# Staging the loads, splitting the denominator off and halving the first chunks in a fused attention and MLP kernel

## The chip, the cores and the metric

The kernel runs on one core of a Trainium2 chip. A core has five engines that run side by side and meet only at semaphores: PE (matrix multiply, TensorE), DVE (VectorE), ACT (ScalarE), POOL (GpSimd) and SP, which here only issues transfers. Each engine takes its instructions in the order of its own queue. Transfers between device memory and the on-chip memory are issued by SP, ACT or POOL and run on 16 DMA engines that all three share. The metric is the device time of one execution in microseconds; lower is better.

## The reference

Inputs are q, k and v of shape (4 batches, 4 heads, 1088 positions, 32), two small sketch matrices S1 and S2 (8 x 32), and the MLP weights w_in (128 x 2048) and w_out (2048 x 128). All are float32.

```python
def phi(x):                       # 8 x 8 products of two sketches: 64 features
    a = einsum('rd,bhsd->bhsr', S1, x)
    b = einsum('rd,bhsd->bhsr', S2, x)
    return einsum('bhsi,bhsj->bhsij', a, b).reshape(*x.shape[:-1], 64)
q_p, k_p = phi(q), phi(k)
kv = einsum('bhsf,bhsd->bhfd', k_p, v)
z = sum(k_p, axis=2)
num = einsum('bhsf,bhfd->bhsd', q_p, kv)
den = einsum('bhsf,bhf->bhs', q_p, z) + 1e-6
x = (num / den) as 4352 tokens x 128 (heads side by side)
out = square(relu(x @ w_in)) @ w_out
```

Nothing of a batch's queries can be finished before all of its keys are summed, since `kv` and `z` run over all 1088 positions. The MLP then works token by token.

## The kernel before, in words

**The order.** A string, `ORDER`, lists some 500 operations by hand. A loop at the end calls them one by one, and each call pins its instructions, so every engine executes its own share of the list in the list's order. An item such as `R.0.3@A` is an operation, its indices and the engine (A for ACT, V for DVE, G for POOL). DMA loads at the top of the kernel are not pinned: the framework places them in their queue, and gives every DMA one of eight lanes (semaphores), so that a later DMA of a lane waits for the earlier one to land.

**Keys of batch b.** `kT` (L212, L218) transposes the loaded k on DVE. `ka` (L233) multiplies it by the sketches on PE, in two groups, 0 and 1, of 4 and 4.5 column blocks. `kc` (L251) copies the result from PSUM on ACT. `kp` (L262) forms the 64 products on DVE. `kv` (L280) sums products times v on PE, and in the same accumulation sums a 32 x 32 product of the two sketches (L290), from which the denominator weights come. `kt` (L302, L309) copies both sums out, `kr` (L315) transposes the first, and in the same operation a matmul with S2 (L324) turns the second into denominator weights. `kx` (L334) and `wc` (L338) put them into `KV` and `Wq`.

**Queries of batch b.** `qT` (L352, L358) transposes q on DVE. `qa` (L380) multiplies by `Wq`, which holds S1, the denominator weights and S2 side by side, in two halves. `qc` (L392) copies to SBUF. `dt`, `dr`, `da` (L400, L407, L412, L419) compute the denominator, its reciprocal and the divided sketch. `qf` (L432) forms the 64 products, `qp` (L445) transposes them. `nd` (L469) multiplies by `KV` on PE, `xe` (L484) casts the result to bfloat16.

**MLP.** Eight chunks of 512 tokens, two for each batch, and a ninth of 256 for the positions that are left over. For each chunk there are eight steps u: `M` (L492) multiplies by two blocks of w_in, `R` (L506 on ACT, L508 on DVE) takes the ReLU from PSUM, `S` (L515 on ACT, L517 on DVE) squares it, `O` (L527) multiplies by w_out and accumulates. `E` (L539) copies the sum out of PSUM and SP stores it (L545; the last chunk L555, in eight small DMAs on SP and ACT).

**Loads.** SP issues k and q of all four batches one after the other (L142, L143), with S1 ahead of them (L116). POOL issues v of batch 0 in four heads and two remainders (L131, L136), then w_in and w_out (L146, L148, converted to bfloat16 on the way), then v of the other batches.

Of the kernel before, what the change touches and what calls it, by code (L numbers as in the profile page):

```python
# [30 lines left out]

ORDER = """
kT.0 ka.0.0 kc.0.0@A ka.0.1 kc.0.1@A kp.0.0 kp.0.1 kv.0.0 kv.0.1 qT.0 kt.0@A kr.0 kx.0@A kT.1
wc.0 qa.0.0 qc.0.0@A qa.0.1 qT.1 qc.0.1@A ka.1.0 ka.1.1 kc.1.0@A dt.0.0@V dr.0.0 da.0.0@V
dt.0.1@V qf.0.0 dr.0.1 da.0.1@V kc.1.1@A qf.0.1 qp.0.0 qp.0.1 nd.0.0 kp.1.0 kv.1.0 xe.0.0@A
M.0.0 R.0.0@A M.0.1 kp.1.1 qT.2 kv.1.1 kt.1@A R.0.1@V S.0.0@V M.0.2 R.0.2@A kr.1 wc.1 S.0.1@V
kT.2 M.0.3 nd.1.0 xe.1.0@V kx.1@A R.0.3@A S.0.3@V S.0.2@A M.0.4 R.0.4@A M.0.5 qa.1.0 qa.1.1
qc.1.0@V R.0.5@A dt.1.0@V qc.1.1@A S.0.4@V dr.1.0 dt.1.1@V da.1.0@V dr.1.1 ka.2.0 ka.2.1 M.0.6
qf.1.0 S.0.5@A R.0.6@A M.0.7 R.0.7@A O.0.0 kc.2.1@A S.0.6@V O.0.1 O.0.2 da.1.1@G M.1.0 M.1.1
O.0.3 O.0.4 R.1.0@A M.1.2 qp.1.0 qf.1.1 qp.1.1 R.1.1@A S.0.7@V O.0.5 R.1.2@A S.1.0@V O.0.6  # L40
kc.2.0@A kp.2.0 M.1.3 M.1.4 R.1.3@A R.1.4@A kp.2.1 nd.2.0 S.1.1@V O.0.7 E.0@A M.1.5 R.1.5@A
S.1.2@V M.1.6 S.1.4@V O.1.0 kv.2.0 kv.2.1 xe.2.0@A R.1.6@A S.1.6@V O.1.1 M.2.0 kt.2@A R.2.0@A
S.2.0@A kr.2 O.1.2 S.1.3@V M.1.7 R.1.7@A wc.2 M.2.1 R.2.1@A kx.2@V qa.2.0 qa.2.1 qc.2.1@A kT.3
ka.3.0 S.1.5@A O.1.3 M.2.2 qc.2.0@V dt.2.0@V dr.2.0 da.2.0@V kc.3.0@A R.2.2@A dt.2.1@G M.2.3
R.2.3@A O.1.4 O.1.5 O.1.6 S.1.7@V O.1.7 qf.2.0 E.1@A S.2.1@V M.2.4 R.2.4@A M.2.5 R.2.5@A S.2.5@A
O.2.0 nd.3.0 dr.2.1 da.2.1@V ka.3.1 M.2.6 R.2.6@A M.2.7 R.2.7@A qf.2.1 kc.3.1@A qp.2.0 S.2.2@V
O.2.1 S.2.3@V O.2.2 O.2.3 xe.3.0@V S.2.4@V M.3.0 R.3.0@A M.3.1 kp.3.0 S.2.6@V O.2.4 O.2.5 O.2.6
S.2.7@V R.3.1@A M.3.2 O.2.7 M.3.3 qp.2.1 S.3.1@A kp.3.1 S.3.0@V E.2@A nd.4.0 R.3.3@A R.3.2@A
xe.4.0@V S.3.3@A kv.3.0 kv.3.1 M.3.4 S.3.2@V M.3.5 O.3.0 O.3.1 kt.3@A kr.3 qT.3 R.3.4@A kx.3@V
wc.3 M.4.0 R.4.0@V S.3.4@V R.3.5@A S.3.5@V M.4.1 R.4.1@A S.4.1@A qa.4.0 qc.4.0@A qa.3.0 qa.3.1  # L50
M.3.6 qc.3.0@V O.3.2 dt.3.0@V dr.3.0 R.3.6@A M.3.7 R.3.7@A O.3.3 O.3.4 S.4.0@V qc.3.1@A M.4.2
S.3.6@V da.3.0@G R.4.2@A M.4.3 R.4.3@A S.3.7@V O.3.5 dt.3.1@V dr.3.1 qf.3.0 qp.3.0 O.3.6 S.4.2@V
S.4.3@V O.3.7 E.3@A da.3.1@G qf.3.1 qp.3.1 M.4.4 dt.4.0@G nd.5.0 R.4.4@A M.4.5 M.4.6 xe.5.0@A
R.4.5@A R.4.6@A O.4.0 O.4.1 M.4.7 R.4.7@A S.4.4@V O.4.2 O.4.3 M.5.0 R.5.0@A M.5.1 R.5.1@V nd.6.0
M.5.2 xe.6.0@V S.4.5@A R.5.2@A S.4.6@V M.5.3 R.5.3@A S.5.0@V O.4.4 O.4.5 S.4.7@V dr.4.0 da.4.0@G
S.5.3@V M.5.4 R.5.4@A O.4.6 M.5.5 S.5.1@V R.5.5@A O.4.7 E.4@V M.5.6 S.5.5@V R.5.6@A S.5.2@V
qf.4.0 nd.7.0 xe.7.0@A M.5.7 R.5.7@A M.6.0 R.6.0@A O.5.0 O.5.1 S.5.4@V M.6.1 R.6.1@A O.5.2 M.6.2
R.6.2@A S.5.6@V O.5.3 O.5.4 M.6.3 S.5.7@V R.6.3@A qp.4.0 M.6.4 S.6.1@A O.5.5 R.6.4@V O.5.6 M.6.5
S.6.0@V O.5.7 M.7.0 R.6.5@A nd.8.0 E.5@V R.7.0@A M.6.6 M.7.1 S.6.2@V O.6.0 S.6.4@A S.6.3@V O.6.1
R.6.6@A S.6.6@A O.6.2 R.7.1@V M.7.2 R.7.2@A S.6.5@V M.6.7 xe.8.0@A O.6.3 O.6.4 O.6.5 S.7.1@V  # L60
M.7.3 R.7.3@A R.6.7@V S.6.7@V O.6.6 M.7.4 S.7.0@V S.7.2@V O.6.7 E.6@V R.7.4@A M.7.5 nd.8.1
R.7.5@A S.7.3@V M.7.6 S.7.5@V xe.8.1@A M.7.7 R.7.7@V O.7.0 O.7.1 O.7.2 R.7.6@A S.7.4@A M.8.0
M.8.1 S.7.7@V R.8.1@V R.8.0@A S.7.6@A O.7.3 O.7.4 M.8.2 M.8.3 S.8.1@V R.8.3@A S.8.0@A O.7.5
O.7.6 R.8.2@V S.8.2@V M.8.4 R.8.4@A M.8.5 R.8.5@V S.8.5@V O.7.7 E.7@A M.8.6 R.8.6@V M.8.7
S.8.3@A O.8.0 O.8.1 O.8.2 O.8.3 S.8.4@V O.8.4 R.8.7@A S.8.7@A S.8.6@V O.8.5 O.8.6 O.8.7 E.8@A
# [4 lines left out]
def kernel(  # L70
# [11 lines left out]
    nc = tc.nc  # L82
# [7 lines left out]
    W = 3 * r  # L90
# [10 lines left out]
    qab_pool = pool("qab", 3)  # L101
# [3 lines left out]
    r_pool = pool("r", 6)  # L105
    g_pool = pool("g", 6)
# [9 lines left out]
    nc.sync.dma_start(out=S12[:r, 0, :], in_=S1)  # L116
# [11 lines left out]
    def load_v(b):  # L128
        for h in range(H):
            vr = v[b, h].rearrange("(t j) d -> t j d", j=NJ)[:, : 4 * NLO, :]  # L130
            nc.gpsimd.dma_start(  # L131
                out=vraw[b][:, h, :NLO, :],
                in_=vr.rearrange("t (i l) d -> i t (l d)", i=4),
            )
        for j2 in range(2):
            nc.gpsimd.dma_start(  # L136
                out=vraw[b][32 * j2 : 32 * (j2 + 1), :, NLO, :],
                in_=v[b].rearrange("h (t j) d -> j t h d", j=NJ)[32 + j2],
            )

    for b in range(B):
        nc.sync.dma_start(out=kin_t[b], in_=k[b].rearrange("h (t j) d -> (h t) j d", j=NJ))  # L142
        nc.sync.dma_start(out=qin_t[b], in_=q[b].rearrange("h (t j) d -> (h t) j d", j=NJ))  # L143
    load_v(0)
    w_in_sb = consts.tile([128, C_TILES, 128], BF16)
    nc.gpsimd.dma_start(out=w_in_sb, in_=moe_w_in.rearrange("d (ct c) -> d ct c", c=128))  # L146
    w_out_sb = consts.tile([128, C_TILES, 128], BF16)
    nc.gpsimd.dma_start(out=w_out_sb, in_=moe_w_out.rearrange("(ct c) d -> c ct d", c=128))  # L148
    for b in range(1, B):
        load_v(b)  # L150


    mask = consts.tile([128, H], F32)
# [9 lines left out]
    dts = [consts.tile([128, 16, r + 1], F32, name=f"dt{i}") for i in range(3)]  # L163
# [5 lines left out]
    for i in (1, 3):  # L169
        pin(nc.vector.memset(kabs[i][64:, :, 4 * H :], 0.0))  # L170
        pin(nc.vector.memset(kps[i][64:, 4 * H :], 0.0))
    for b in range(B):
        pin(nc.vector.memset(vraw[b][64:, :, NLO, :], 0.0))
    KV = consts.tile([128, B, 2, 128], F32)
    qT_rem = consts.tile([128, B, 64], F32)
    pin(
# [5 lines left out]
    nc.tensor.transpose(  # L182
        T_ps[:, : 2 * r], S12.rearrange("r h d -> r (h d)"), ident[: 2 * r, : 2 * r]
# [10 lines left out]
    Wq = consts.tile([128, B, H, W], F32)  # L194
# [7 lines left out]
    T = {}  # L202

# [65 lines left out]

    def kv(b, gi, eng):  # L270
        if gi == 0:
            T["acc", b] = ps_m.tile([128, 512], F32, tag="m", name="acc_ps")
        acc = T["acc", b]
        t, s = T["kp", b, gi], T["kab", b, gi]
        P = 128
        for m in range(4 + gi):
            first, last = gi == 0 and m == 0, gi == 1 and m == 4
            for h in range(H):
# [3 lines left out]
                        vraw[b][:P, h, 4 * gi + m, :],  # L282
                        t[:P, m * H + h].rearrange("p i j -> p (i j)"),
                        start=first,
                        stop=last and h > 0,
                    )
                )
            a, b2 = (s[:P, x, m * H : m * H + H].rearrange("p h i -> p (h i)") for x in range(2))
            pin(
                nc.tensor.matmul(  # L290
                    acc[:32, 64:96],
                    b2,
                    a,
                    start=False,
                    stop=last,
                )
            )

    def kt(b, eng):
# [9 lines left out]
        pin(COPY[eng](Gs[:32, b], T["acc", b][:32, 64:96]))  # L309

    def kr(b, eng):
        T["kr", b] = t = ps_m.tile([128, 512], F32, tag="m", name="kr_ps")
        for f in range(2):
# [21 lines left out]

    def wc(b, eng):
        pin(
            nc.vector.tensor_tensor(  # L338
                out=Wq[:, b, :, r : 2 * r],
                in0=T["acc", b][:, 96:128].rearrange("p (h x) -> p h x", h=H),  # L340
                in1=mask[:, :, None].to_broadcast([128, H, r]),
                op=ALU.mult,
            )
        )
# [20 lines left out]
    def groups(b):  # L365
        return 4 if b < 4 else 2

    def qa(b, i, eng):
        T["qq", b, i] = t = ps_m.tile([128, 512], F32, tag="m", name="qab_ps")
        for m in range(groups(b)):  # L370
            for c in range(2):
# [4 lines left out]
                else:  # L376
# [4 lines left out]
                        t[64 * c : 64 * c + 64, m * H * W : (m + 1) * H * W],  # L381
# [6 lines left out]

    def qc(b, i, eng):
        n = groups(b) * H  # L390
# [206 lines left out]
```

## Time and profile before

| | us |
|---|---|
| three timed runs | 128.24, 129.75, 130.01 |
| their median | 129.75 |
| the profiled execution | 128.9 |
| its span on the core | 127.1 |
| DVE busy | 101.9 (80% of the span) |
| PE busy | 100.2 (79%) |
| ACT busy | 87.1 (69%) |
| POOL busy | 22.6 (18%) |

The span is the time from the first to the last instruction of the core. Busy time of PE is modelled, since its matmuls overlap in a pipeline; a busy PE need not be a PE at full speed. The chain that ended last is found by going back from the last instruction, at each step to whatever released it. By line it is 14% `M` (L492), 13% `O` (L527), 10% the loads of v and 9% squaring on DVE (L517). A row of the page gives the granted clock of PE over the span in 40 slices; it is at 9 tenths or more except in four slices between about 25 and 38 us, where it reads 6, 5, 5 and 7.

### The profile page before, as it was taken

What the parts mean: (1) busy time and instruction counts of PE and PEld (TensorE: products, weight loads), DVE (VectorE), ACT (ScalarE), POOL (GpSimd) and SP (SyncE); (2) the same over time, 40 slices, a digit from 0 to 9 for tenths busy, and PEclk for the clock granted to TensorE, in tenths of its full rate; (3) what the DMA queues carried; (4) which work ended last, traced back from release to release, by engine and by line L of the source; (5) the groups of instructions that cost most, each with busy time, mean ns of one, the idle gap of its engine ahead of it and who ended that gap; (6) DMA issues with size and microseconds to landing.
All of it is one profiled execution on the core that took longest, in us unless ns stands there. A gap on an engine that the chain in (4) does not pass through costs nothing.

```text
span 127.1 us, 4039 instructions
## 1 busy us (share of the span) xinstructions
PE 100.2 (79%) x1729; PEld 72.7 (57%) x1729; DVE 101.9 (80%) x187; ACT 87.1 (69%) x130; POOL 22.6 (18%) x38
## 2 busy tenths in 40 slices
PE   0062187307999998999998999999899999799920
PEld 0061086303576874878766687767376767669810
DVE  6359304999569999999999998999999799879800
ACT  4220003400449998989999997999799999599910
POOL 6934252049700120001000000240010000000000
PEclk9999999965579999999999999999999999999997
DMA  2999999965610000210030020002002003020121
GB/s 71 330 273 263 294 282 295 221 113 136 138 41 5 0 5 0 66 25 5 0 83 5 21 67 0 5 17 65 5 0 62 26 9 81 1 65 23 33 66 27
DMA packets 7953, 10.24 MB, mean 81 GB/s; under 512 B 4864, under 2 KB 5248, under 8 KB 7936
## 3 DMA queue, kind: packets, MB, share of 16 engines
q1 hardware_dynamic: 2896, 6.62, 18.0%
q0 software_dynamic: 4768, 3.30, 13.9%
q8 instruction: 13, 0.21, 0.8%
q10 hardware_dynamic: 272, 0.07, 0.2%
q14 instruction: 4, 0.03, 0.1%
HBM read 8.79 MB, written 2.23 MB: 87 GB/s over the span
## 4 chain that ended last, share of the span: by engine, by line
PE 39%; DVE 30%; DMA 10%; issue 8%; ACT 6%; POOL 2%; POOLq 0%; ACTq 0%; DVEq 0%
PE h_ps L492 14%; PE o_ps L527 13%; DMA v_in<-in_v_dram 10%; DVE g_sb L517 9%; PE acc_ps L280 5%; DVE qf L432 5%; PE nd_ps L469 4%; ACT r_sb L506 4%; DVE qp L445 4%; DVE kp L262 2%; DVE kT L212 2%; POOL v_in L131 2%; PE kr_ps L315 1%; DVE rec L412 1%; DVE den L407 1%
## 5 line engine op out<-in xcount | busy, mean ns | idle before, releaser
L506 ACT ACTIVATE r_sb<-h_ps 128x1024 bf16<-128x1024 f32 (+1 forms) x61 | 58.4, 1005 | 6.0 <-PE h_ps L492 4.7
L492 PE MATMUL h_ps<-xT,w_in_sb 128*128 128x512 bf16 (+1 forms) x144 | 38.8, 375 | 0.8 <-ACT r_sb L506 0.7
L527 PEld LDWEIGHTS <-g_sb 128*128 128x128 bf16 x544 | 33.1, 98 | 8.1 <-DVE g_sb L517 0.9
L527 PE MATMUL o_ps<-w_out_sb,g_sb 128*128 128x128 bf16 x544 | 36.6, 219 | 0.4 <-DVE g_sb L517 0.4
L517 DVE TENSOR_TENSOR g_sb<-r_sb 128x1024 bf16<-128x1024 bf16 (+1 forms) x55 | 35.0, 668 | 0.5 <-ACT r_sb L506 0.3
L492 PEld LDWEIGHTS <-w_in_sb 128*128 128x128 bf16 x144 | 12.1, 100 | 9.7 <-issue 4.5
L515 ACT ACTIVATE g_sb<-r_sb 128x1024 bf16<-128x1024 bf16 (+1 forms) x17 | 16.8, 985 | 0.2
L469 PE MATMUL nd_ps<-qp,KV 32*32 32x256 f32 (+1 forms) x384 | 11.1, 340 | 6.7 <-DVE qp L445 6.7
L280 PE MATMUL acc_ps<-kp,v_in 128*32 128x64 f32 x288 | 10.5, 270 | 6.2 <-DMA v_in<-in_v_dram 5.4
L131 POOL DMA_DIRECT2D v_in<-in_v_dram x16 | 11.2, 706 | 15.3 <-DMA v_in<-in_v_dram 7.5
L508 DVE TENSOR_SCALAR r_sb<-h_ps 128x1024 bf16<-128x1024 f32 (+1 forms) x11 | 11.3, 1027 | 3.0 <-PE h_ps L492 3.0
L280 PEld LDWEIGHTS acc_ps<-kp,v_in 128*32 128x32 f32 x288 | 8.2, 127 | 9.2 <-DMA v_in<-in_v_dram 6.2
L469 PEld LDWEIGHTS nd_ps<-qp,KV 32*32 32x32 f32 x384 | 5.4, 108 | 11.6 <-issue 8.5
L262 DVE TENSOR_TENSOR kp<-kab 128x1024 f32<-128x1024 f32 (+1 forms) x12 | 10.7, 943 | 1.5 <-ACT kab L251 1.5
L419 POOL TENSOR_TENSOR aq<-qab,rec 128x128 f32<-128x128 f32 (+1 forms) x4 | 3.7, 914 | 42.4 <-DVE rec L412 42.4
L445 DVE STREAM_TRANSPOSE qp<-qf 128x1024 f32<-128x1024 f32 (+1 forms) x9 | 10.5, 1176 | 0.1
L432 DVE TENSOR_TENSOR qf<-aq,qab 128x1024 f32<-128x1024 f32 (+1 forms) x9 | 10.3, 1142 | 0.1
L302 ACT COPY kvT<-acc_ps 128x256 f32<-128x256 f32 x4 | 1.5, 375 | 11.4 <-PE acc_ps L290 11.4
L290 PE MATMUL acc_ps<-kab 128*32 128x32 f32 x72 | 8.9, 223 | 0.0
L233 PE MATMUL kab_ps<-Wk,kT 128*64 128x64 f32 x136 | 6.0, 246 | 3.1 <-DVE kT L212 3.1
L484 ACT CAST xT<-nd_ps 128x256 bf16<-128x256 f32 (+1 forms) x12 | 3.3, 328 | 7.5 <-PE nd_ps L469 7.5
L290 PEld LDWEIGHTS acc_ps<-kab 128*32 128x32 f32 x72 | 8.0, 142 | 0.0
(53 smaller groups left out, 77.7 us busy)
## 6 DMA issues: line engine op xcount, KB each, us to landing
k_in<-in_k_dram SPq DMA_DIRECT2D x4, 544.0 KB, 9.5
q_in<-in_q_dram SPq DMA_DIRECT2D x4, 544.0 KB, 5.6
v_in<-in_v_dram POOLq DMA_DIRECT2D x16, 128.0 KB, 8.2
out_dram<-osb SPq DMA_DIRECT2D x32, 64.0 KB, 1.7
w_in_sb<-in_moe_w_in_dram POOLq DMA_DIRECT2D x1, 512.0 KB, 15.1
w_out_sb<-in_moe_w_out_dram POOLq DMA_DIRECT2D x1, 512.0 KB, 20.1
v_in<-in_v_dram POOLq DMA_DIRECT2D x8, 16.0 KB, 7.3
S2bd<-in_S_dram ACTq DMA_DIRECT2D x4, 1.0 KB
```

Of the source, the lines that this page charges most:

```text
L131: nc.gpsimd.dma_start(out=vraw[b][:, h, :NLO, :], in_=vr.rearrange("t (i l) d -> i t (l d)", i=4),)
L262: nc.vector.tensor_tensor(out=t[:P, g0:g1], in0=s[:P, 0, g0:g1, :, None].to_broadcast([P, g1 - g0, r, r]), in1=s[:P, 1, g0:g1, None, :].to ...
L280: nc.tensor.matmul(acc[32 * h : 32 * h + 32, :64], vraw[b][:P, h, 4 * gi + m, :], t[:P, m * H + h].rearrange("p i j -> p (i j)"), start=first,
L290: nc.tensor.matmul(acc[:32, 64:96], b2, a, start=False, stop=last,)
L432: nc.vector.tensor_tensor(out=t[:, :n], in0=T["aq", b, i][:, :n, :, None].to_broadcast([128, n, r, r]), in1=s[:, :n, None, 2 * r :].to_bro ...
L445: nc.vector.transpose(T["qp", b][:, :, 128 * i : 128 * i + 32 * nm].rearrange("p f (m t) -> p m f t", t=32), T["qf", b, i][:, : nm * H].re ...
L469: nc.tensor.matmul(nds[l][32 * h : 32 * h + 32, c0:c1], KV[rows, be, f, 32 * h : 32 * h + 32], src[rows, 2 * h + f, c0:c1], start=(f == 0) ...
L492: nc.tensor.matmul(t[:, i, :N], w_in_sb[:, 2 * u + i, :], T["x", ci][:, :N], start=True, stop=True,)
L506: pin(nc.scalar.activation(t[:, :, :N], h[:, :, :N], ACTF.Relu))
L515: pin(nc.scalar.activation(t[:, :, :N], s, ACTF.Square))
L517: pin(nc.vector.tensor_mul(t[:, :, :N], s, s))
L527: nc.tensor.matmul(T["o", ci][:, m, :], T["g", ci, u][:, i, m * 128 : (m + 1) * 128], w_out_sb[:, ct, :], start=(ct == 0 and m == 0), stop ...
```

## The change

**Loads.** k of batch 0 is the first load of SP, and S1 moves to ACT. Of v of batch 0, head 0 goes on SP behind k, head 1 on ACT, heads 2 and 3 and the two remainders on POOL, with w_in behind them. `hold` is a copy of one element on POOL from a tensor that has to land first into a tensor that is loaded later; the later load overwrites the element and so has to wait for the copy. One hold puts k of batch 1 behind head 3 of v of batch 0, the other puts k of batch 2 behind w_out. q has no hold, and neither has k of batch 3. In the built program SP's queue is: k0, head 0 of v0, q0, q1, q2, k3, q3, k1, k2. POOL's is: two heads of v0, its remainders, w_in, the hold for k1, w_out, v1, the hold for k2, v2, v3.

**Denominator weights.** The 32 x 32 sums leave `kv` for an operation of their own, `kg`, with a PSUM tile of their own; `gs`, `wz` and `wc` follow it. They need the copied sketches (`kc`) but neither the products (`kp`) nor v.

**Batch 0 in halves.** `kT.0` comes in two parts, so that `ka.0.0` can follow the first. The chunks 0 and 1 are now made of one half of the columns each (`qp.0.0` feeds chunk 0, `qp.0.1` chunk 1), and their output rows alternate in memory.

**Zero matmuls.** `W.n` multiplies a zero tile by itself, 128 x 512 in bfloat16, n times, into a PSUM tile that nobody reads. Four stand ahead of the transpose of the sketches, ten more in the list.

**Smaller pieces.** `kp` is one instruction for both parts of group 1. `dt`, `dr` and `da` handle both halves of a batch at once, except for batch 0, and none of them runs on POOL any more. ReLU outputs and squares lie in tiles of two steps, and `S` with the engine letter M squares both in one instruction of 128 x 2048: of the 72 squarings, 10 are on ACT (17 before), 24 single ones on DVE (55 before), and 19 double ones on DVE. Nine ReLUs are on DVE (11 before). All nine `qc` are on ACT (6 before). The last chunk is stored with four DMAs. The whole of `ORDER` is a new list.

```diff
+    def load_v(b, h, dma):
+        if h < H:
+            vr = v[b, h].rearrange("(t j) d -> t j d", j=NJ)[:, : 4 * NLO, :]
+            dma.dma_start(out=vraw[b][:, h, :NLO, :],
+                in_=vr.rearrange("t (i l) d -> i t (l d)", i=4))
...
+    def load(b, dst, src):
+        nc.sync.dma_start(out=dst[b], in_=src[b].rearrange("h (t j) d -> (h t) j d", j=NJ))
+    def hold(dst, src):
+        pin(nc.gpsimd.tensor_copy(dst[:1, 0, :1], src[:1, 0, :1]))
+    load(0, kin_t, k)
+    load_v(0, 0, nc.sync)
+    load_v(0, 1, nc.scalar)
+    load(0, qin_t, q)
+    for h in range(2, H + 2):
+        load_v(0, h, nc.gpsimd)
     w_in_sb = consts.tile([128, C_TILES, 128], BF16)
     nc.gpsimd.dma_start(out=w_in_sb, in_=moe_w_in.rearrange("d (ct c) -> d ct c", c=128))
+    hold(kin_t[1], vraw[0][:, H - 1])
+    load(1, kin_t, k)
+    load(1, qin_t, q)
     w_out_sb = consts.tile([128, C_TILES, 128], BF16)
     nc.gpsimd.dma_start(out=w_out_sb, in_=moe_w_out.rearrange("(ct c) d -> c ct d", c=128))
+    for h in range(H + 2):
+        load_v(1, h, nc.gpsimd)
+    hold(kin_t[2], w_out_sb)
+    for b in (2, 3):
+        load(b, kin_t, k)
+        load(b, qin_t, q)
...
+    def W(n, eng):
+        for _ in range(n):
+            pin(nc.tensor.matmul(T["idle"], idle[:, :128], idle, start=True, stop=True))
...
+    def kg(b, eng):
+        T["gg", b] = gg = ps_m.tile([128, 512], F32, tag="m", name="gg_ps")
+        for m in range(9):
+            s, g0 = T["kab", b, m // 4 if m < 8 else 1], (m % 4 if m < 8 else 4) * H
+            a, b2 = (s[:, x, g0 : g0 + H].rearrange("p h i -> p (h i)") for x in range(2))
+            pin(nc.tensor.matmul(gg[:32, :32], b2, a, start=(m == 0), stop=(m == 8)))
...
     def SQ(ci, u, eng):
+        i, n = (0, 4) if eng == "M" else (2 * (u % 2), 2)
+        t = pair("g", g_pool, ci, u)[:, i : i + n, :N]
+        s = pair("r", r_pool, ci, u)[:, i : i + n, :N]
...
-    kT.0 ka.0.0 kc.0.0@A ka.0.1 kc.0.1@A kp.0.0 kp.0.1 kv.0.0 kv.0.1 qT.0 kt.0@A kr.0 kx.0@A kT.1
-    wc.0 qa.0.0 qc.0.0@A qa.0.1 qT.1 qc.0.1@A ka.1.0 ka.1.1 kc.1.0@A dt.0.0@V dr.0.0 da.0.0@V
...
+    kT.0.0 ka.0.0 kT.0.1 ka.0.1 kc.0.0 kp.0.0 kc.0.1 W.2 kg.0 gs.0 qT.0 W.1 wz.0 wc.0 W.1 qa.0.0
+    qc.0.0@A kv.0.0 kp.0.1 kv.0.1 kt.0 dt.0.0 dr.0.0 qa.0.1 kr.0 da.0.0 qf.0.0 qp.0.0 qc.0.1@A
+    dt.0.1 dr.0.1 kx.0@A W.5 nd.0.0 xe.0.0@A W.1 nd.0.1 xe.0.1@A kT.1.0 ka.1.0 kc.1.0 M.0.0 R.0.0@A
+    ka.1.1 kc.1.1 M.0.1 M.0.2 R.0.1@A da.0.1 R.0.2@A qf.0.1 qp.0.1 nd.1.0 xe.1.0@A kg.1 gs.1 M.0.3
+    qT.1 S.0.0@V S.0.1@V O.0.0 R.0.3@A M.0.4 R.0.4@A kp.1.1 wz.1 wc.1 nd.1.1 kT.2.0 M.0.5 O.0.1
...
```

## The prediction

> **What bounds the kernel now.** The page comes first, for the span: 127.1 us in an execution of 128.9 us, so 1.8 us lie around it. That execution lies inside the three timed runs (128.24 to 130.01, median 129.75), 0.85 below their median. The sum below is made against 128.9. Changes under about 2% can't be told from none on this kernel.
>
> The chain that ended last, in order of time (start, length, work):
>
> ```profile
> 3.87 12.52 DMA v_in<-in_v_dram
> ...
> 19.35 0.38 ACT kvT L302
> ...
> 20.66 0.20 DVE Wq L338
> 20.91 0.91 PE qab_ps L380 x16
> ...
> 25.79 1.23 DVE qf L432
> ...
> 29.45 1.96 PE nd_ps L469 x32
> ...
> 32.83 1.82 PE h_ps L492 x4
> ```
>
> For the first 33 us there is no MLP. The last head of v lands at 16.4 us, and then everything is in series: key sums, transposes, denominator weights, query features, numerators. The first ReLU (`R.0.0`) runs at 33.83. Windows over 33.8 to 122 us, summed, show the rest:
>
> ```profile
> sum 88.20, PE 85.83 PEld 61.54 DVE 80.53 ACT 80.86 POOL 4.71; mean PE 5.72 PEld 4.10 DVE 5.37 ACT 5.39 POOL 0.31
> ```
>
> This MLP phase has three nearly full engines: 81 us of work each on DVE and ACT in 88.2 us. So the kernel is a start of 33.8 us, a phase of 88.2, and a tail of 5.1. The start can shrink; the phase only if work leaves DVE and ACT together.
>
> Why v is late: the first five SP loads, and for k the time from issue to landing (shortest/median/longest of the three that are known):
>
> ```profile
> 1.19 0.37 SPq L142 DMA_DIRECT2D k_in<-in_k_dram  x1
> 1.60 0.42 SPq L143 DMA_DIRECT2D q_in<-in_q_dram  x1
> 2.45 0.33 SPq L142 DMA_DIRECT2D k_in<-in_k_dram  x1
> 2.83 0.94 SPq L143 DMA_DIRECT2D q_in<-in_q_dram  x1
> 5.55 0.33 SPq L142 DMA_DIRECT2D k_in<-in_k_dram  x1
> ```
>
> ```profile
> DMA to landing us min/median/max: 4.3/9.5/13.4
> ```
>
> With issues at 1.19, 5.55 and 7.21 that is k0 at 5.5, k2 at 15.05, k3 at 20.6. The tile answers give q0 at 7.2, v0's heads at 9.3, 11.5, 14.1 and 16.4, w_in at 20.8, w_out at 26.3. The DMA row is at 9 from 3 us on. So from 7.2 to 20.6 SP's queue moves five 544 KB tensors (k1, q1, k2, q2, k3), **2.7 us each**, while POOL's moves a head of v in about 2.4.
>
> **The start of the changed kernel, step by step.** k0 is issued 0.45 us earlier (S1 has left SP), so it lands near 5.05. Then:
> - `kT.0.0` is half of the 1.23 us transpose, 0.68: 5.75. `ka.0.0`, 16 of the 34 instructions that took 2.0 us: 6.8. `kc.0.0` 0.37: 7.25. `kp.0.0` 1.21: 8.5. `qT.0` 1.56: 10.1. Beside it: `ka.0.1`, `kc.0.1` (8.4), `kg.0` (18 instructions, about 1 us: 9.5), `gs.0` 0.17, `wz.0` 0.16. `wc.0` on DVE ends at 10.4; before it was 20.86, behind v. Here splitting the denominator off pays.
> - `qa.0.0` about 0.65, `qc.0.0` 0.49: 11.7. `kp.0.1` as one instruction of 1280 columns, 1.5 from 1.21 for 1024: 11.9.
> - v0: heads 2 and 3 are the first two on POOL's queue, so by the old heads 0 and 1 at 9.3 and 11.5; heads 0 and 1 go by SP and ACT, ahead of q0. `kv.0` fits behind `kp.0.1`: PE 12 to 13.4. `kt.0`, `kr.0`, `kx.0`: 0.37, 0.7, 0.37, done by 15.0, hidden behind DVE.
> - DVE: `dt` 0.28, `dr` 0.55, `da` 0.29, `qf` 1.20, `qp` 1.24: 15.5. `nd.0.0` (half the columns) 0.55 to 1.0, `xe.0.0`; `nd.0.1`, `xe.0.1`: xT complete near 17.7. DVE does `dt`, `dr` to 16.4.
>
> If nothing else intervened, `kT.1.0` (1.23), `ka.1.0` and `M.0.0` would give the first ReLU at 18.7. But the DVE, PE and ACT orders all put batch 1's keys ahead of it: `kT.1.0`, `ka.1.0`, `kc.1.0`. In the built program SP holds k0, v0's head, q0, q1, q2, k3, q3, **k1**, k2: only k1 and k2 carry the hold, and the unheld loads went past them. So k1 has the place that k3 had: five tensors behind q0. Before, that place landed at 20.6. Now q0 lands at 7.2 again (k0 0.45 earlier, head 0 of v about 0.4 between them), and 5 x 2.7 gives **20.6**. The hold itself (head 3 at 11.5) is earlier than the queue reaches k1, so it costs nothing. DVE stands from 16.4 to 20.6, with `da.0.1`, `qf.0.1`, `qp.0.1` behind `kT.1.0`; PE stands with `M.0.0` behind `ka.1.0`. Then `kT.1.0` to 21.9, `ka.1.0` to 22.9, `M.0.0` to 23.75: first ReLU at **23.8**, 10.0 us earlier than now.
>
> What else is queued behind a wait. On ACT the third small load of S2bd now waits for k0 (both use one DMA lane in the built program); behind it are the four `Wq` copies, 0.68 us, done by 5.9, ahead of `kc.0.0` at 6.8: no cost. On POOL the first hold is a copy of one element; POOL's nearest rows are 0.3 (128x64 product) and 1.0 (128x128), and a gain is excluded. Behind it stands the issue of w_out, then at about 12, which w_in's transfer (until about 16, by 20.8 less 4.8) covers. On SP, q2, k3 and q3 wait for early lanes (head 0, q0, head 1 of v), all landed by 7.5 while the queue is still at q1. The outputs of batch 0 go out in rows of 512 B instead of 2 KB; the only row is 1.7 us for a 64 KB DMA; doubled or not, it ends tens of us before the end.
>
> Zero matmuls: 14 of 128x512. PE's clock row reads 0.50 from 29.4 to 33.0 after an idle stretch of 6 us, and two matmuls of this size then take 0.86 against 0.43 later. So 14 cost 3.0 to 6.0 us of PE, all in waits (four before the first transpose, ten between 8 and 17); I take no cost. If `W.5` runs at half clock it ends after `qp.0.0` and costs 1 us, which the wait for k1 hides. None lies in the wait for k1 itself, 17.2 to 21.9, so I took `ka.1.0` and `M.0.0` at half speed (0.9 us; 0 if the clock holds). [...]
>
> [...]
>
> **The second gate.** k2's hold waits for w_out. POOL's queue has two heads (4.8 us) fewer ahead of it, so 26.3 becomes 21.5; k2, with an empty SP queue, takes k0's 4.3: 25.8. DVE needs it at `kT.2.0`. From 20.6: `kT.1` 1.4, `da`, `qf`, `qp` 2.7, `qT.1` 1.5, two squarings 1.3, `kp.1.1` 1.45, `wc.1`: about 29.3. Cost 0; at w_out's old 26.3 it would cost 1.3. v1 follows w_out and is needed near 32.
>
> **The phase.** DVE: 2 ReLUs fewer (-2.4), 7 squarings more (+4.9), 18 pairs in one instruction (0.69 and 0.42 for 1024 and 512 columns give 1.24 for 2048: -0.15 each by the means, -0.05 by the 1.90 us that three in a row took; -0.9 to -2.7, I take -1.8), evictions and casts (2 x 0.69, net 6 x 0.41 less 2 x 0.2, 3 x 0.56: -5.1), denominators in larger pieces and POOL's six pieces taken over (-0.4), `kp` and memsets (-0.6): 101.9 to about 96.5. ACT: +2.1, -7.4, +1.5 (`qc`), +1.2 (`E`), +2.6 (`xe`): 87.1, as before. Ahead of 23.8 DVE has done some 15.4 and ACT 6.3, which leaves 81.1 and 80.8, against 80.5 and 80.9 in the old phase. So the phase keeps its length, +0.6 for DVE. In its first 6.2 us DVE was busy for 4.1 and ACT for 4.4; in my walk ACT runs without gaps from 23.8, -1.2. Sum **87.6**. PE inherits 2.3 us (`ka.1.1`, part of `kv.1`, `M.0.0`) and loses its half-clock stretch to 37; 0 taken.
>
> Tail: the last output goes out in two DMAs per queue instead of four. SP's four took 2.5, ACT's 2.8 of issue; half saved, 5.1 becomes 3.9.
>
> Sum: 23.8 + 87.6 + 3.9 = 115.3 us of span, +1.8 = **117.1**; against the median perhaps 0.8 more. I forecast 117.
>
> **Rivals.**
> - Forecast, k1 at about 20.6: 117 (115 to 119.5). Chance 0.50.
> - k1 in time, because SP's queue drains faster without four heads of v beside it: first ReLU at 18.7, 112. For it: less small traffic early. Against: w_in and w_out then share. 0.18.
> - Second gate late: POOL's queue lands w_out at 26 or later and k2 at 31 to 34, while `kT.2.0` heads DVE and `ka.2.0` stands ahead of `M.1.0`: 2 to 5 us, plus the phase's paired squarings letting `O` wait: 120 to 125. 0.18.
> - Slower: the first gate. k1 stands behind everything, and each us past 20.6 is one of the total. From L = 32.4 the change is no gain, from 35 it is over 2% slower (131 or more). It needs SP's queue at half its old rate, 5.4 us a tensor. Against: POOL's 4.8 us less of v. 0.08.
> - Loads as late as now and the rest even: 126 to 129. 0.06.
>
> The range reaches from the second case to the third: 111.5 to 124.5. Faster by over 2%: 0.86; within: 0.06; slower: 0.08.
>
> **What would show it.** First ReLU near 23.8; DVE waiting for a k load around 16 to 20.6 at `kT`; `wc` near 10.4; no wait at `kT.2.0`; 87 to 89 us from first ReLU to the last eviction. I am wrong if k1 lands by 17 or after 23, or if that phase is not 85 to 91 us.

## The result, and the profile after

| | before | after |
|---|---|---|
| four timed runs each, us | 128.24 to 130.01 | 123.5 to 125.7 |
| their median | 129.52 | 124.83 |
| the profiled execution | 128.9 | 124.32 |
| its span | 127.1 | 122.5 |
| first ReLU (`R.0.0`) starts | 33.83 | 30.80 |
| from there to the end of the last eviction | 88.1 | 87.6 |
| from there to the end of the span | 5.2 | 4.1 |

The changed kernel takes 0.962 of the time before (95% interval 0.949 to 0.974). Executions over 1.5% longer than the shortest of their kernel are left out of every ratio and interval here. The change is faster, but the gain is 4.7 us and not the forecast 12; 124.83 lies just above the range. Phase and tail are as predicted (87.6 and 4.1, where 87.6 and 3.9 were forecast). The first ReLU is 7.0 us later than predicted, and 124.32 less 117.1 is 7.2: the whole miss lies ahead of the MLP.

The page of the changed kernel: its engines, and the rows of the span in 40 slices of 3.06 us.

```profile
PE 104.1 (85%) x1807; PEld 75.1 (61%) x1807; DVE 96.8 (79%) x153; ACT 86.4 (71%) x138; POOL 17.1 (14%) x32
...
PE   6094009993999999999999999999999999999950
...
DVE  5360225938989999999999999998999799699810
...
PEclk9999655699599999999999999999999999999999
DMA  3999899968723000004013003000300300303032
```

PE has two holes after its first work, in slices 5 and 6 (12 to 18 us) and in slice 10, and DVE is nearly as empty in slices 4 to 6 and 9. The trace's records of the clock begin at 10.0 us: full to 13.4, half from there to 23.7, half again from 30.5 to 33.9. Before the first record the row shows 9 although nothing is recorded there. DMA is busy all through the first hole. What the engines wait for there is in the waits (engine, tile, line, releaser: total, times, longest, us):

```profile
PE gg_ps L320 <- DMA S2bd<-in_S_dram: 7.4, 1, 7.4
...
DVE qT L388 <- DMA q_in<-in_q_dram: 5.4, 1, 5.4
```

and the chain that ended last (start, length, work) puts them in order:

```profile
2.47 14.95 DMA S2bd<-in_S_dram
...
17.52 10.45 DMA k_in<-in_k_dram
...
28.07 1.25 DVE kT L248
...
29.46 0.69 PE kab_ps L271 x16
30.15 0.61 PE h_ps L558 x2
```

So two transfers make up 25.4 of the first 28 us. S2bd is four loads of 1 KB on ACT's queue, which hold the sketch S2 for the denominator weights. They were issued from 2.47 on and landed at 17.4, 15 us later. Then k1 was issued, and landed at 27.98. Of before the chain named v and then a series of small steps.

SP's issues (start, length from first to last issue, work):

```profile
0.73 0.42 SPq L145 DMA_DIRECT2D k_in<-in_k_dram  x1
1.21 0.71 SPq L133 DMA_DIRECT2D v_in<-in_v_dram  x1
1.97 9.11 SPq L145 DMA_DIRECT2D q_in<-in_q_dram  x3
14.56 0.33 SPq L145 DMA_DIRECT2D k_in<-in_k_dram  x1
17.08 0.33 SPq L145 DMA_DIRECT2D q_in<-in_q_dram  x1
17.52 9.35 SPq L145 DMA_DIRECT2D k_in<-in_k_dram  x2
```

The first line is k0, the third q0, q1 and q2, then k3, q3, and in the last k1 and k2. SP stands for lanes: q2 goes out at 10.8, when head 0 of v (the second line) has landed; k3 at 14.56, when q0 has; q3 at 17.08, when head 1 of v has landed from ACT's queue; k1 at 17.52, next behind q3. The chain names S2bd for k1, since k1 has its lane and S2bd landed last, at 17.42; but q3 had held the queue until 17.41, so without S2bd k1 would have gone out about 0.1 us earlier. What both waited for is head 1: it holds up q3 by its lane, and S2bd stands behind it on ACT's queue. Until 14.56 k3 and q3, which go ahead of k1, had not even been issued.

The timeline of DVE (start, length, work, and in brackets the idle time before it and its releaser):

```profile
14.57 1.30 DVE L388 STREAM_TRANSPOSE qT<-q_in 128x512 f32<-128x512 f32 x2 [5.44 <-DMA q_in<-in_q_dram]
...
28.07 1.25 DVE L248 STREAM_TRANSPOSE kT<-k_in 128x1024 f32<-128x1024 f32 x1 [2.29 <-DMA k_in<-in_k_dram]
```

and on ACT the first ReLU:

```profile
30.80 1.02 ACT L578 ACTIVATE r_sb<-h_ps 128x1024 bf16<-128x1024 f32 x1 [0.24 <-PE h_ps L558]
```

`kT.1.0` is where the prediction put the last wait of the start, and the walk from there on is 0.5 us shorter than predicted (2.73 us to the ReLU against 3.2), but it begins at 28.07 instead of 20.6. In the phase, windows over 30.8 to 118.4 us sum to what was forecast, with DVE and ACT at 82.0 and 80.3 (81.1 and 80.8 predicted):

```profile
sum 87.60, PE 87.02 PEld 63.76 DVE 81.96 ACT 80.26 POOL 3.55; mean PE 29.00 PEld 21.25 DVE 27.32 ACT 26.75 POOL 1.18
```

### The profile page after: what moved, and what is told of

It is laid out like the page before. It is cut to its first block, busy times and chain, and to the rows that moved or that the text cites. A ratio compares the mean times of both kernels' runs of the same rounds, so it can differ in the third digit from the quotient of the medians.

```text
span 122.5 us, 4127 instructions
## 1 busy us (share of the span) xinstructions
PE 104.1 (85%) x1807; PEld 75.1 (61%) x1807; DVE 96.8 (79%) x153; ACT 86.4 (71%) x138; POOL 17.1 (14%) x32
## 4 chain that ended last, share of the span: by engine, by line
PE 64%; DMA 21%; ACT 8%; DVE 2%; issue 1%; DVEq 0%; SPq 0%
PE h_ps L558 24%; PE o_ps L601 22%; DMA S2bd<-in_S_dram 12%; DMA k_in<-in_k_dram 9%; PE nd_ps L528 7%; ACT r_sb L578 6%; PE kab_ps L271 3%; PE qab_ps L416 2%; PE acc_ps L346 2%; PE gg_ps L313 2%; DVE kT L248 1%; ACT g_sb L589 1%; PE kr_ps L370 1%; ACT osb L613 1%; ACT qab L433 0%
## 5 line engine op out<-in xcount | busy, mean ns | idle before, releaser
L591 DVE TENSOR_TENSOR g_sb<-r_sb 128x1024 bf16<-128x1024 bf16 (+2 forms) x43 | 36.8, 885 | 1.4 <-PE o_ps L601 0.9
L433 ACT COPY qab<-qab_ps 128x384 f32<-128x384 f32 (+1 forms) x9 | 4.1, 480 | 11.1 <-PE qab_ps L416 11.0
L528 PE MATMUL nd_ps<-qp,KV 32*32 32x256 f32 (+2 forms) x448 | 11.2, 298 | 0.0
L580 DVE TENSOR_SCALAR r_sb<-h_ps 128x1024 bf16<-128x1024 f32 (+1 forms) x9 | 8.8, 984 | 1.8 <-PE h_ps L558 1.8
L388 DVE STREAM_TRANSPOSE qT<-q_in 128x512 f32<-128x512 f32 x8 | 5.2, 684 | 5.4 <-DMA q_in<-in_q_dram 5.4
L589 ACT ACTIVATE g_sb<-r_sb 128x1024 bf16<-128x1024 bf16 (+1 forms) x10 | 9.1, 940 | 0.1
L271 PEld LDWEIGHTS kab_ps<-Wk,kT 128*64 128x64 f32 x136 | 6.1, 171 | 4.3 <-issue 2.7
L416 PE MATMUL qab_ps<-Wq,qT 128*64 128x96 f32 x128 | 7.4, 274 | 0.0
L416 PEld LDWEIGHTS qab_ps<-Wq,qT 128*64 128x64 f32 x128 | 6.5, 157 | 1.1 <-DVE Wq L331 0.5
L248 DVE STREAM_TRANSPOSE kT<-k_in 128x1024 f32<-128x1024 f32 (+1 forms) x5 | 5.0, 1017 | 2.3 <-DMA k_in<-in_k_dram 2.3
## 6 DMA issues: line engine op xcount, KB each, us to landing
q_in<-in_q_dram SPq DMA_DIRECT2D x4, 544.0 KB, 12.6
```

The source lines that it names most:

```text
L271: nc.tensor.matmul(kk[64 * c : 64 * c + 64, m * 64 : (m + 1) * 64], kt[:, c0 + 64 * c : c0 + 64 * c + 64], Wk.rearrange("p h x -> p (h x)" ...
L416: nc.tensor.matmul(t[64 * c : 64 * c + 64, m * H * W3 : (m + 1) * H * W3], cols, Wq[:, be].rearrange("p h x -> p (h x)"), start=True, stop ...
L528: nc.tensor.matmul(nds[l][32 * h : 32 * h + 32, d0 : d0 + n], KV[rows, be, f, 32 * h : 32 * h + 32], src[rows, 2 * h + f, c0 : c0 + n], st ...
L589: pin(nc.scalar.activation(t, s, ACTF.Square))
L591: pin(nc.vector.tensor_mul(t, s, s))
```

## The experiments

Each run is one edit. The intervals are of the ratio to the kernel before, on the same chip; before had medians of 128.04 to 129.16 us beside e1 to e10, so kernels of different rows are best compared by their ratios. Span and first ReLU are of one profiled execution; those of e2, e7 and e10 took 0.7 to 1.3 us more than the median of their kernel, so for these three the span says less than the median.

| run | edit | first ReLU | to last eviction's start | span | median | ratio, interval |
|---|---|---|---|---|---|---|
| changed kernel | | 30.80 | 87.2 | 122.5 | 124.83 | 0.962, 0.949 to 0.974 |
| e1 | heads 0, 1 of v0 on POOL | 23.44 | 87.4 | 115.0 | 115.81 | 0.907, 0.895 to 0.918 |
| e2 | v by quarters, same queues | 24.45 | 87.2 | 116.1 | 117.05 | 0.916, 0.905 to 0.926 |
| e3 | S2bd ahead of head 1 | 28.12 | 85.8 | 118.5 | 120.88 | 0.946, 0.936 to 0.956 |
| e4 | k1 not held | 29.98 | 85.8 | 120.3 | 122.66 | 0.962, 0.950 to 0.974 |
| e5 | e1, k1 not held | 22.33 | 87.0 | 113.5 | 115.46 | 0.901, 0.892 to 0.910 |
| e6 | e5, no zero matmuls | 21.82 | 87.1 | 113.1 | 116.29 | none |
| e7 | e5, squares single | 25.21 | 85.8 | 115.2 | 116.35 | 0.899, 0.883 to 0.915 |
| e8 | e5, v by quarters on POOL | 20.18 | 88.3 | 112.7 | 114.26 | 0.891, 0.881 to 0.902 |
| e9 | e8, k2 not held either | 20.33 | 87.0 | 111.5 | 114.41 | 0.886, 0.879 to 0.893 |
| e10 | e9, denominators behind kv | 25.23 | 87.4 | 116.9 | 117.41 | 0.898, 0.891 to 0.906 |

**e1: v on POOL alone.** The theory after the traces: the two heads of v on SP and ACT, 128 KB each, clog these queues, and everything behind them slips. If so, sending them by POOL must bring back the predicted start.

```diff
-    load_v(0, 0, nc.sync)
-    load_v(0, 1, nc.scalar)
     load(0, qin_t, q)
-    for h in range(2, H + 2):
+    for h in range(H + 2):
         load_v(0, h, nc.gpsimd)
```

> Heads 0 and 1 of v of batch 0 go back to POOL's queue; all else is the changed kernel. Theory A (a load of a head of v, whose source has 4 as its outermost dimension, keeps only a few of the 16 DMA engines busy; on SP and ACT it holds up whatever shares those engines and queues): the small S2bd loads land before 7 us instead of 17.4, the zero-column wait of wz goes, q0 lands near 7.5 instead of 14.6, k1 near 20.6 instead of 28, first ReLU near 24, span about 115.5. Theory B (the DMA engines are simply full and the first gate and the order of the loads set the landing times): q0 and k1 land within 2 us of the changed kernel's 14.6 and 28, first ReLU 29 to 31, span 121 to 123.

The first ReLU starts at 23.44 (23.8 had been predicted for the change itself), and the span is 115.0 (115.3 predicted). Timeline of DVE in e1, with `wc.0` and `kT.1.0`:

```profile
10.98 0.19 DVE L329 TENSOR_TENSOR Wq<-gg_ps,mask 128x32 f32<-128x32 f32 x1 [0.61 <-PE gg_ps L318]
...
20.79 1.25 DVE L246 STREAM_TRANSPOSE kT<-k_in 128x1024 f32<-128x1024 f32 x1 [3.39 <-DMA k_in<-in_k_dram]
```

`wc.0` runs at 10.98 instead of 18.78, q0 is read at 8.95 without a wait, and k1 lands 0.2 us from the predicted 20.6. SP issues k1 only at 14.13, when the hold lets it, but 591 of the 768 packets of the six loads ahead of it had started by then, so the queue had not reached k1 and the hold cost nothing, as predicted. Two lines of the change cost 7.4 us of the start, and 7.5 us of the span.

**e2: the same queues, another shape.** Is it the queue, or the way that a head is cut? A head's load has 4 as its outermost dimension (4 x 32 rows of 1 KB). Here each of the four loads takes a quarter of the positions of all heads, which makes it 32 x 4 rows of 1 KB: the same bytes, rows, number of loads and queues, for all batches.

```diff
-            vr = v[b, h].rearrange("(t j) d -> t j d", j=NJ)[:, : 4 * NLO, :]
+            vr = v[b].rearrange("h (t j) d -> t h j d", j=NJ)
             dma.dma_start(
-                out=vraw[b][:, h, :NLO, :],
-                in_=vr.rearrange("t (i l) d -> i t (l d)", i=4),
+                out=vraw[b][32 * h : 32 * h + 32, :, :NLO, :].rearrange("p h l d -> p h (l d)"),
+                in_=vr[:, :, NLO * h : NLO * h + NLO, :].rearrange("t h l d -> t h (l d)"),
```

> Same queues, same bytes, same 1 KB rows, but each of the four v loads of a batch now takes a quarter of the positions of all heads (32 x 4 x 256) instead of all positions of one head (128 x 1 x 256, read as 4 x 32 x 256). Theory A: outermost dimension 32 instead of 4 spreads it over 16 engines, so head loads on SP and ACT cost about 0.4 us each; S2bd lands before 8, q0 near 8, k1 near 20, first ReLU 22 to 24, span 114 to 116. Rival C (1 KB rows on SP's and ACT's queues lose against 4 KB rows of the others, whatever their shape): no change, v's first load on SP lands near 10.8, S2bd near 17, first ReLU near 30.8, span 122 to 123.

The first ReLU is at 24.45: 6.3 of the 7.4 us come back with SP and ACT still carrying half of v. `kT.1.0` stands where it does in e1:

```profile
20.93 1.25 DVE L248 STREAM_TRANSPOSE kT<-k_in 128x1024 f32<-128x1024 f32 x1 [2.39 <-DMA k_in<-in_k_dram]
```

Most of the 1.0 us to e1 lies behind it: from `ka.1.0` to the ReLU it is 2.13 us against 1.26, with PE at half clock from 20.6 us on in this execution (the 16 matmuls of `ka.1.0` take 1.12 us, 0.69 in e1). SP's issues in e2:

```profile
1.20 0.42 SPq L133 DMA_DIRECT2D v_in<-in_v_dram  x1
1.66 4.10 SPq L145 DMA_DIRECT2D q_in<-in_q_dram  x3
10.09 0.33 SPq L145 DMA_DIRECT2D k_in<-in_k_dram  x1
10.47 0.44 SPq L145 DMA_DIRECT2D q_in<-in_q_dram  x1
11.02 13.10 SPq L145 DMA_DIRECT2D k_in<-in_k_dram  x2
```

q2 goes out at 5.4 instead of 10.8, and k1 at 11.0 instead of 17.5. (The edit also loosens the hold on k1, since the element that it copies now comes with the first quarter: the copy runs at 5.47 instead of 12.43, and w_out is issued behind it at 5.59 instead of 12.55. That puts more traffic beside k1, not less.) The trace's records of single packets show why. In both kernels the load of v on SP is 128 packets of 1 KB, and one of them takes 46 ns in the median.

| v load | first packet to last, us | most of its packets at once |
|---|---|---|
| SP, a head (changed kernel) | 5.57 | 6 |
| SP, a quarter (e2) | 1.23 | 17 |
| ACT, a head (changed kernel) | 10.73 | 3 |
| ACT, a quarter (e2) | 4.91 | 5 |

So a head has fewer packets under way at once than a quarter, and its 128 packets take 4.5 times as long on SP (5.57 / 1.23) and 2.2 times on ACT. Besides its data each load leaves packets of 4 bytes in its queue: up to 34 us there are 132 in SP's queue in the changed kernel and 144 in e2, which is 16 for each of the eight loads of k and q, 4 for the head and 16 for the quarter; in ACT's queue there are 52 and 64, again 12 fewer. Both the counts, 4 against 16, and the ratio of 4.5 would fit a head on a fourth of the engines that a quarter of v keeps busy. That is the author's estimate: on how many engines a load ran, which they were, and whether the two heads met on them, no run here shows. The edit also changes which partitions a load writes (32 instead of 128), and nothing here separates this from the outermost dimension of the source.

**e3: S2bd first.** What is S2bd's lateness worth? The memset and the four small loads move ahead of head 1 on ACT's queue.

```diff
+    S2bd = consts.tile([128, H, D], F32)
+    pin(nc.vector.memset(S2bd, 0.0))
+    for h in range(H):
+        nc.scalar.dma_start(out=S2bd[r * h : r * h + r, h, :], in_=S2)
...
     load_v(0, 0, nc.sync)
     load_v(0, 1, nc.scalar)
```

> The four 1 KB loads of S2bd stand ahead of v's head on ACT's queue; all else is the changed kernel. If the wait of wz for S2bd alone is what made the start late: first ReLU near 24, span near 116. Theory A: S2bd lands by 7 and wz no longer waits, but q0 (14.6) still holds wc until about 16.3 and k1 (28) still holds the first MLP step: first ReLU 29.5 to 31, span 121 to 123.

A miss, on the good side: span 118.5. `wz.0` no longer waits and `wc.0` runs at 12.84, but `kv.0` meets the same head itself. Timeline of PE in e3:

```profile
19.88 2.14 PE L346 MATMUL acc_ps<-kp,v_in 128*32 128x64 f32 x70 [4.92 <-DMA v_in<-in_v_dram]
```

The order of the small loads is worth 2.7 us of the start, but that is not S2bd alone. Head 1 is itself issued later, at 4.64 instead of 1.77, and q0 lands earlier, at 11.47 instead of 14.55. The lanes turn with the order, too: q3 now waits for head 0 (9.44) and no longer for head 1, k1 goes out at 11.56, when the hold lets it, instead of 17.52, and `kT.1.0` no longer waits. The expectation had left q0 and k1 where they were.

**e4: k1 not held.** The prediction saw the danger of the changed kernel in k1's place in the queue. Here the hold on k1 goes and nothing else, so that k1 follows q0.

```diff
-    hold(kin_t[1], vraw[0][:, H - 1])
     load(1, kin_t, k)
```

> Without the hold on k1: SP's queue is then k0, v's head, q0, k1, q1, q2, k3, q3, k2. If k1's place in the queue is what ends last in the start: k1 lands 8 to 11 us earlier, near 18, and the first ReLU moves by as much. Theory A: k1 is there near 18, but wz still waits for S2bd until 17.4, so DVE reaches the keys of batch 1 at 25.8 and the first ReLU comes at 28 to 29; span 119.5 to 121.

k1 is issued at 2.45 and read at 27.27 without a wait, and yet the first ReLU is only 0.8 us earlier (29.98); the ratio is that of the changed kernel. Timeline of PE in e4:

```profile
19.70 0.60 PE L319 MATMUL gg_ps<-Gs,S2bd 128*128 128x32 f32 x2 [9.21 <-DMA S2bd<-in_S_dram]
```

S2bd lands later still, at 19.50 against 17.42, and takes the place of k1. (Without the hold POOL issues w_out at 4.90 instead of 12.55, so there is more traffic beside it; no run tells what that adds.) Undoing the gate, the suspect of the prediction, is no remedy while the heads are there.

**e5: e1 without the hold on k1.** With the heads on POOL k1 is what ends last in the start (3.39 us of wait). What is behind it?

> v of batch 0 all on POOL and no hold on k1, so that SP's queue is k0, q0, k1, q1, q2, k3, q3, k2. If k1 (20.8 in the run with v on POOL) is what ends last in that start: k1 lands near 10, DVE takes the keys of batch 1 at 17.4, and the last cast of chunk 0 (20.9 there) ends last instead; first ReLU 20.5 to 21.5, 2 to 3 us earlier, span 111.5 to 113. If the hold kept the way free for v and w_in: v's last head lands later than 13.9 and eats 1 us or more of it; span 113 to 115.

`kT.1.0` runs at 18.00 without a wait, the first ReLU at 22.33: of the 3.39 us 1.1 remain, a miss by about a microsecond. Behind k1 stands chunk 0 itself, whose second cast runs at 20.76, because `kv.0` still waits for the last head of v (until 14.12). The medians, 115.46 and 115.81 (ratios 0.901 and 0.907), do not tell the two apart.

**e6: no zero matmuls.** In e5 the 14 matmuls on the zero tile are left out; nobody reads their result.

```diff
     def W(n, eng):
-        for _ in range(n):
+        for _ in range(0):
```

> The same without the fourteen zero matmuls. My prediction took them as free and of no use but for the clock: 3 to 6 us of PE work in waits. If they keep the clock up: PE's clock row reads half speed somewhere between 9 and 25 us, kv and nd of batch 0 take 0.5 to 1 us longer each, first ReLU 0.5 to 2 us later than in the run with them; span 0.5 to 2 us longer. If they do nothing: within 0.3 us.

The 66 matmuls of `kv.0` that come last take 2.13 us without them and 1.19 with them (e5), `qa.0.1` 1.55 and 0.88, and `kT.1.0` runs at 19.09 instead of 18.00. The trace's first record of a full clock is at 17.63 without them and at 11.10 with them. So with them PE is at full clock earlier. The first ReLU is nevertheless at 21.82, half a microsecond earlier, and the span 113.1 against 113.5. The chain that ended last in e5 shows why:

```profile
14.12 1.19 PE acc_ps L343 x66
...
16.76 1.08 PE idle_ps L203 x5
...
18.44 0.32 PE idle_ps L203
...
21.34 0.95 PE h_ps L555 x2
```

The zero matmuls (`idle_ps`) stand on it themselves, with 1.40 us, which is nearly the 1.6 us that they save on `kv.0` and `qa.0.1`. And `M.0.0` (`h_ps`) falls on a stretch of half clock in e5 (21.34 to 24.75) and takes 0.95 us there, 0.54 in e6. The four times of e6, 114.7, 115.0, 117.6 and 118.8, lie on both sides of e5's 115.3 to 116.2: no gain or loss in time is shown.

**e7: squares one by one.** The 19 double squarings (18 of 128x2048 and one half as wide, of the last chunk) become two single ones each.

```diff
-        i, n = (0, 4) if eng == "M" else (2 * (u % 2), 2)
+        if eng == "M":
+            SQ(ci, u - 1, "V")
+            eng = "V"
+        i, n = 2 * (u % 2), 2
```

> As the run with v on POOL and k1 free, but the 19 squarings of a pair are two instructions each (128 x 1024). My term for pairing them was 1.8 us of DVE (0.9 by the spacing in a row, 2.7 by the means): DVE busy 0.9 to 2.7 us more; span 0.5 to 2 us longer if DVE bounds the phase, within 0.5 if the phase is bound by PE and ACT.

Groups of DVE in e5 and then e7, by shape (count, busy time, mean ns of one, idle time before):

```profile
L588 DVE TENSOR_TENSOR g_sb<-r_sb 128x2048 bf16<-128x2048 bf16 x18 | 21.7, 1212 | 1.1 <-PE o_ps L598 0.9
L588 DVE TENSOR_TENSOR g_sb<-r_sb 128x1024 bf16<-128x1024 bf16 x22 | 14.5, 680 | 1.7 <-ACT r_sb L575 1.5
```

```profile
L591 DVE TENSOR_TENSOR g_sb<-r_sb 128x1024 bf16<-128x1024 bf16 x57 | 36.0, 680 | 1.2 <-PE o_ps L601 0.7 <-ACT r_sb L575 0.6
```

By the means a pair saves 2 x 680 - 1212 = 148 ns, 2.7 us in 18. But DVE's busy time grew only from 96.5 to 97.4, 0.9 us, since instructions in a row overlap at their ends (57 of 680 ns would be 38.8 us end to end, and 36.0 are busy): the low end of the predicted 0.9 to 2.7. The time shows none of it (0.899 against 0.901). The first ReLU of the profiled execution is late because v landed late in it (the last head at 16.04 against 14.07) and `kv.0` then ran at half clock (0.50 from 15 to 20 us; its last 66 matmuls took 2.13 us, 1.19 in e5).

**e8: v by quarters on POOL, k1 not held.** Both findings together: e5 with the v loads of e2.

> As the run with v on POOL and k1 free, but v loaded by quarters of the positions (outermost dimension 32). Theory A: on POOL's queue too a load by heads keeps few DMA engines busy (one head in 2.1 to 2.4 us); by quarters v of batch 0 is complete by 9 instead of 13.9 and kv of batch 0 no longer waits for it; the first ReLU gains at most 1 us, since DVE's chain to qp of batch 0 does not wait for v: span 111 to 113. If POOL's queue spreads any shape over all engines: v lands at 13.9 as before, no change.

The last quarter of v0 lands at 11.83, not by 9, but before `kv.0` asks for it (12.46, no wait), and the first ReLU is at 20.18. Now a gate binds, the second. Timeline of DVE in e8:

```profile
28.37 1.25 DVE L245 STREAM_TRANSPOSE kT<-k_in 128x1024 f32<-128x1024 f32 x1 [2.77 <-DMA k_in<-in_k_dram]
```

This is `kT.2.0`; k2 was issued at 24.16, behind w_out, and landed 4.2 us later. At 0.891 of the time before, where the changed kernel takes 0.962, e8 beats both kernels of the change.

**e9: no gate left.** e8 without the hold on k2.

> The kernel with v by quarters on POOL and k1 unheld, and now the hold on k2 gone too (no gate is left). Gates cost more than they give: k2 is issued by SP near 7 to 9 us instead of 24.2, kT.2.0 loses its wait of 2.77, and the first ReLU stays at 20 to 21: span 110 to 112, median 112 to 113.5. Rival, the gate did its work: k2 beside v, w_in and w_out makes k1 or v0 later, so that the first ReLU goes to 22 or later and what the wait gives is lost at the start: span 112.5 to 114.

`kT.2.0` runs at 26.11 without a wait, and the start is as early as in e8 (20.33): w_in and v do not need the protection. w_out does lose by it, about a microsecond (24.75 against 23.82), and the first `O` now waits for it. Timeline of PE in e9:

```profile
24.79 0.61 PE L598 MATMUL o_ps<-w_out_sb,g_sb 128*128 128x128 bf16 x8 [0.97 <-DMA w_out_sb<-in_moe_w_out_dram]
```

The same wait is 0.19 in e8. The profiled span is 1.2 us shorter, 111.5, but the medians are 114.41 and 114.26 (ratios 0.886 and 0.891, with intervals that overlap). As a gain over e8 this can't be told from nothing, as a loss neither: no worth of the second gate is shown.

**e10: denominators behind kv.** In e9, `kg.0`, `gs.0`, `wz.0` and `wc.0` of batch 0 go back behind `kt.0`, as they stood before the change.

```diff
-kp.0.0 kc.0.1 W.2 kg.0 gs.0 qT.0 W.1 wz.0 wc.0 W.1 qa.0.0 qc.0.0@A kv.0.0 kp.0.1 kv.0.1 kt.0
+kp.0.0 kc.0.1 W.2 qT.0 W.1 W.1 kv.0.0 kp.0.1 kv.0.1 kt.0 kg.0 gs.0 wz.0 wc.0 qa.0.0 qc.0.0@A
```

> The same kernel as the one without any gate, but batch 0's denominator weights (kg, gs, wz, wc) stand behind kv.0 and kt.0 again, as in the kernel before; the queries of batch 0 follow them. If the split of the denominator pays once its transfers are there, wc.0 ends near 15.5 to 16 instead of 11.6, the first ReLU comes 3 to 4.5 us later and the span is 2.5 to 4.5 us longer than without the edit. Rival, the start is bound by the loads of k1 anyway: first ReLU under 1.5 us later, span under 1 us longer.

Timeline of DVE in e10:

```profile
15.40 0.19 DVE L328 TENSOR_TENSOR Wq<-gg_ps,mask 128x32 f32<-128x32 f32 x1 [3.17 <-PE gg_ps L317]
...
21.58 1.19 DVE L245 STREAM_TRANSPOSE kT<-k_in 128x1024 f32<-128x1024 f32 x1
```

`wc.0` comes 4.0 us later than in e9 (15.40, 11.38), `kT.1.0` 3.8 us later, still without a wait for k1, and the first ReLU 4.9 us later, with PE at half clock from about 22 to 29 us in this execution. So at the start the split pays, by the forecast 3 to 4.5 us and a little more. At the end less is left: the ratios are 0.898 and 0.886, about 1.6 us, under 2%, with intervals that just meet. In the changed kernel the split could hardly pay: there the same `wc.0` waited for S2bd.

## Why the prediction missed, point by point

- **What bounds the kernel before** (start, phase, tail): right. The change moved the start, and phase and tail came out within 0.2 us.
- **"Heads 0 and 1 go by SP and ACT, ahead of q0", "head 0 of v about 0.4 between them"**: this is the step that failed. 0.4 us was the author's estimate, and no run shows it: the packets of head 0 took 5.57 us on SP, and those of a quarter of v, which is the same 128 KB, 1.23 (e2). The prediction's own rows spoke against 0.4: POOL's queue needed about 2.4 us for a head, and SP's 2.7 us for a tensor of 544 KB, over four times the size. q0 behind head 0 landed at 14.57 and not at 7.2. e1 and e2 show it from both sides: with another queue the sum of the prediction holds (115.0 of span in e1 against 115.3), and with another shape nearly (116.1 in e2, in an execution 0.9 us above the median of its kernel).
- **"S2bd ... no cost"**: only the lane was looked at, not what stood ahead of S2bd in ACT's queue: head 1, landing at 17.08. `wc.0` came at 18.78, not at 10.4. With S2bd ahead of head 1 the start is 2.7 us shorter (e3), though not by S2bd alone.
- **"All landed by 7.5"** (the lanes for which q2, k3 and q3 wait): 10.8, 14.56 and 17.08, by the same cause. Lanes turned one late load into late issues of loads that have nothing to do with it, and k1 came out last.
- **k1 at 20.6**: 27.98 in the changed kernel, 20.79 in e1. The count of tensors ahead of it and the rate per tensor gave the right landing as soon as nothing else stood in the queue. But its worth was mis-sized: with that wait of 3.39 us gone, 1.1 us is gained (e5).
- **The rival "k1 in time"** (18.7, 112): it was not what happened, and even with k1 and v both in time (e9) the first ReLU comes at 20.33, since DVE reaches `kT.1.0` at 17.74 and not at 16.4; the start's other steps had been walked 1.3 us too fast there, 0.3 more behind it.
- **The slower rival** (the first gate, SP's queue at half its rate) named the right place. Its condition held in part: the queue did not run slower, it stood still for lanes. It did not reach its point of 32.4; k1 landed 4.4 us ahead of that.
- **The walk behind k1**: 2.73 us from `kT.1.0` to the first ReLU and 2.65 in e1, where 3.2 had been taken with PE at half speed, the author's estimate from the clock of 0.50 after 5.96 us of idle PE in the trace of before. In e1 the clock does fall to half, but only at 23.5 us, when the walk is over. The 0.55 us, less 0.19 by which `kT.1.0` is late, are what e1 lies ahead of the predicted 23.8.
- **The second gate**: no wait in the changed kernel (`kT.2.0` at 36.85), where all else is late. w_out landed at 26.29, its old time, and not at 21.5: that term was 4.8 us too early, and only luck that it cost nothing. With the start repaired it costs a wait of 2.77 us (e8). The rival of 120 to 125 holds the measured time by luck: its condition came true (w_out at 26.29, the last packet of k2 at about 31.5), but the wait that it priced did not come, since DVE reached `kT.2.0` only at 36.85.
- **DVE and ACT**: busy 96.8 and 86.4, forecast 96.5 and 87.1. The pair of squares took 1.215 us (1.24), and e7 puts the worth of pairing at the low bound.
- **Zero matmuls** at no cost: right in the changed kernel, where PE stands idle for 2.08 us behind them until `kT.1.0` is done. With k1 in time they are not free: 1.40 us stand on the chain of e5, about what they save.
- **Three queues**: 0.4 us had been counted for head 0 on SP and nothing for head 1 on ACT. 7.4 us of start were lost (30.80 in the changed kernel, 23.44 in e1). With v by quarters three queues still gave nothing: `kT.1.0` at 20.93 in e2 against 20.79 with all of v on POOL. What goes with the loss is the shape of the load, which stands in the diff and had not been weighed: 6.3 of the 7.4 us came back with quarters on the same queues.

## What to carry to other kernels

Before a load is moved to another issuing engine, compare its shape with those of the loads that are there (128 KB took 5.57 us on SP as 4 x 32 rows and 1.23 as 32 x 4), and count what is queued behind it on that engine, the smallest loads and the lanes too: here one slow load of 128 KB delayed all of them. Price a gate with everything in the queue that passes it, and ask what comes second; here removing the predicted wait gave a third of its length. When a forecast fails in one stage, check whether the others hold: a sum that was right elsewhere tells where to look.

## What the runs showed of the hardware

- Four loads of 1 KB took 15 us to land behind one load of 128 KB in the same queue, while DMA's row stood at 8 or 9. So a 9 in the row did not mean that what was waited for would land soon.
- q0, 544 KB, landed 12.6 us after its issue with head 0 of v ahead of it, and had been read at 8.95 without that (e1).
- The count of 4-byte packets went with the shape of a load on SP's and ACT's queues: 16 for a k, a q or a quarter of v, 8 for a load of eight rows, 4 for a head (132 on SP and 52 on ACT up to 34 us in the changed kernel, 144 and 64 in e2). On POOL's queue it did not: each load left 16 there, heads too (416 for 26 loads before 40 us in e1).
- A 9 in the row of the granted clock can mean that nothing is recorded. The first record is at 10.0 us in the changed kernel, 24.89 in e4, 17.63 in e6 and 19.48 in the kernel before, and the row shows 9 before it. But `kv.0` (72 matmuls), which runs at 22.14 in e4, takes 2.15 us there, as it does at a recorded half clock in the changed kernel, against 1.35 in e8; in e6 66 of them take 2.13. The first `ka` of the changed kernel (34 matmuls) takes 2.18 us, `ka.2` of e1, at full clock, 1.21. So ahead of the first record the duration of a known matmul is the safer sign.
